# Local attention with a gated projection: softmax on halves of 64 query rows

## The chip, the cores and the metric

The kernel runs on one core of one Trainium2 chip. The metric is device time of one execution in microseconds (us). The engines are named as the profile names them: PE is the matrix engine (PEld its weight loads), DVE the vector engine, ACT the scalar engine, POOL the GpSimd engine, SP the queue that issues every DMA. PSUM is the memory that PE writes; it has eight banks of 512 fp32 columns, of which POOL can read none. SBUF is the other on-chip memory.

## What is computed

Attention for 4 batches, 8 heads, 768 positions, head size 64, in which a query sees the first 8 keys ("global") and the last 96 up to itself ("local"), with a bias by distance; then a causal convolution of five taps over positions makes a gate, and the gated projection is projected again.

```python
scores = scale * np.matmul(q, k.transpose(0, 1, 3, 2))
keep = is_global | is_local                       # key < 8, or 0 <= query - key < 96
scores = np.where(keep, scores + bias, -1000000000.0)
a = np.exp(scores - np.max(scores, axis=-1, keepdims=True))
a = a / (np.sum(a, axis=-1, keepdims=True) + 1e-09)
x = np.matmul(a, v)                               # heads side by side: 512 channels
gate = 1.0 / (1.0 + np.exp(-gate_pre))            # gate_pre: 5 causal taps over x
return (gate * (x @ w_val) @ w_out)
```

All inputs are fp32, the three weights are float64 in memory as the kernel gets them.

## The kernel before, in words

A **group** is one batch, one half of the sequence (`hf`, 384 positions) and one pair of heads; there are 32, in the order batch, half, pair. A group has three **steps** `k`, blocks of 128 queries; `s = 3 * g + k` numbers all 96. A step's window is 232 keys for all its 128 queries (96 before the block, 8 global, the block itself); the first step of a sequence needs only its own 128. So 80 steps are full and 16 are first steps.

A group passes through these operations, each a small function:

- `load`, `load_v0`, `load_v`: keys, queries and values by DMA, four buffers each. The window's values come as two tiles of 128 keys (`v`, 104 rows used of one).
- `scores` (S): for each step and head `j` one fp32 matmul, 64 rows of the array deep (head `j` lies on partitions 64 j to 64 j + 63), 128 queries wide, 232 keys long, into four PSUM banks `s`. A matmul has two records in the trace.
- `add_bias` (AM, DVE): scores plus bias to SBUF, with the row minimum. `expo` (EX, ACT): exp and row sum. `guard` (RG) and `recip` (RC): 1 / sum. `norm` (NM, POOL or DVE): the product.
- `transpose` (PT, PE): the probabilities `p` by matmul with the identity into one PSUM bank `pt`: for a full step two of 104 columns and two of 128. `evac_pt` (EV, ACT or DVE): to SBUF as `a`, 464 columns.
- `pv` (PV, PE): per head one matmul over 128 keys and one over 104 into the PSUM bank `x`; head `j` gets columns 64 j to 64 j + 63 of the array.
- `hist_in` (HI) puts the last four positions of the earlier half before `x`; `x_high` and `x_low` (XH, XL) split x into two reduced-precision parts `xh`, `xl`; `conv` (CV) runs five taps on x into `gate`; HO keeps the last four positions for the later half.

There is one bank `x`. For the first `EARLY` = 7 groups, `x_out` (XE) copies x to an SBUF tile `xs` at once, and the taps, XH and XL read that; POOL may then do some of them. From group 7 on they read the bank, which stays taken until they are done.

Four groups make a phase: `sigmoid`, `val` (projection, 48 matmuls of 384 columns), `gated` with `g_high` and `g_low`, `outp` (36 matmuls of 512 columns), `evac_o`, `store`. The eight weight slices are converted from float64 on the way, in about the first 25 steps: `f64_abs` (ACT), then `f64_op` 0 to 4 (operation 0, a clamp, on POOL or DVE; the rest on DVE), `w_high`, `w_rest`, `w_low`.

The order on every engine is fixed when the program is built. A planner (`Plan.order`) keeps for each operation an urgency (in units of steps; the constants `U_...`), the engines that may do it, each with a cost, and what it waits for, and hands out the operations one by one. `plan.ring` makes an operation wait until the n-th older user of a buffer has freed it. `PV` of a group and `S` of the group two later stand together on PE.

Of the kernel before, what the change touches and what calls it, by code (L numbers as in the profile page):

```python
# [8 lines left out]
F32 = mybir.dt.float32  # L9
# [5 lines left out]
ALU = mybir.AluOpType  # L15
AX = mybir.AxisListType
WARM = 8
S_B, PT_B, X_B = 4, 1, 1
# [8 lines left out]
EARLY, XS_B, U_XO, U_CVE = 7, 8, 0.21, 0.5  # L27
# [23 lines left out]
S_AT = {(k, j): (2 * j + k // 2, k % 2) for k in range(3) for j in range(2)}  # L51
# [79 lines left out]
def attention_moe(ctx, tc, qT, kT, kg, vw, v0, v, counts_in, wv, cw, wo, out):  # L131
# [39 lines left out]
    bias = one.tile([P, H, P + WIN], F32, name="bias")  # L171
# [8 lines left out]
    hist = one.tile([P, NP, HIST], F32, name="hist")  # L180

# [18 lines left out]
    def width(s):  # L200
        g, k = divmod(s, HB)
        return P if groups[g][1] == 0 and k == 0 else WIN
# [14 lines left out]
    def load_v(g):  # L217
        b, hf, p = groups[g]
        t = tile_of(("v", g), [P, HB, 2, 2, D], F32, "v", V_B)
        if hf == 0:  # L220
            nc.sync.dma_start(t[:, 1:], vw[b, p, :, : HB - 1])
        else:
            nc.sync.dma_start(t, vw[b, p, :, HB - 1 :])

    for g, (b, hf, p) in enumerate(groups):
# [5 lines left out]
        if hf == 0:  # L231
# [4 lines left out]
        plan.add(key, 3 * g + U_LV + 0.1, {SP: 0.5}, lambda e, g=g: load_v(g),  # L236
                 plan.ring("v", V_B, key, [("PV", g)]), P * (HB - 1 + hf) * 4 * D * 4)
# [11 lines left out]
    plan.add(("WARM",), -100, {PE: 0.43 * WARM}, lambda e: zeros(WARM))  # L249
    for g in range(FILL_TO):  # L250
# [4 lines left out]
    def iotas(e):  # L255
# [7 lines left out]
        nc.gpsimd.tensor_copy(rel[:, CA + NG :], rel0[:, OWN_A:])  # L263
        nc.gpsimd.iota(col, pattern=[[1, P]], base=0, channel_multiplier=0, allow_small_or_imprecise_dtypes=True)
# [35 lines left out]
    def biases(e, h, part):  # L300

        cols = slice(0, P) if part == 0 else slice(P, P + WIN)
        engine(e).tensor_scalar(  # L303
            out=bias[:, h, cols], in0=dist[:, cols], scalar1=-8.0 * 2.0 ** -(h + 1), scalar2=1.0,
# [13 lines left out]
    def f64_op(e, raw, n, nm, k):  # L318
# [4 lines left out]
        if k == 0:  # L323
            engine(e).tensor_scalar(out=y, in0=y, scalar1=F64_MIN, scalar2=1.0, op0=ALU.max, op1=ALU.mult)
# [14 lines left out]
    OPS64 = (0.45, 0.5, 0.7, 0.5, 0.65)  # L339
# [29 lines left out]
    for i in range(2 * NC):  # L369
# [6 lines left out]
        for k in range(5):  # L376
# [5 lines left out]
            plan.add(key, u + 0.1 * k, {DVE: OPS64[k]} if k else {DVE: OPS64[k], POOL: 0.95},  # L382
# [570 lines left out]
```

## Time and profile before

| | |
|---|---|
| runs, us | 320.62, 321.60, 321.67: median 321.6 |
| profiled execution: span, first to last instruction | 319.6 us; no other time is given of it |
| median less span | 2.0 us |
| busy share of the span | PE 90%, PEld 72%, DVE 73%, ACT 73%, POOL 54% |
| mean granted clock of PE | 0.960 |
| the chain that ended last, by engine | PE 59%, DVE 14%, POOL 13%, ACT 4%, no visible wait 4%, DMA 3% |
| DMA | 36.27 MB, 114 GB/s on average |

The busy shares are averages over stages with different limits; the slices of part 2 of the page tell the stages apart. A busy PE is not a PE at its peak: records of matmuls overlap. In the chain of waits a row tells when a piece began, how long it held the end up, and on which line. Groups of instructions are listed as line, engine, operation, output and inputs, shapes and count, then busy time and the mean of one, then the engine's idle time before them.

### The profile page before, as it was taken

Reading aid. Unit: us, or ns where it says so; the run is one execution under the profiler, and the core shown is the slowest. Engines: PE = TensorE matmul, PEld = TensorE weight load, DVE = VectorE, ACT = ScalarE, POOL = GpSimd, SP = SyncE. Lnnn points to the kernel's source line nnn. Section 1 sums busy time; section 2 is a strip of 40 time slices with the busy share of each in tenths; the row PEclk is TensorE's granted clock in tenths of the full one; section 3 lists DMA queues with packets and bytes.
Section 4 is the critical chain, followed back from the end, with each engine's and each line's share of the span. In section 5 each row is a group of like instructions: output and inputs, shape, how many; then the busy total and the mean of one; then the engine's idle time right before and its main releaser. Section 6 shows DMA issues by size and latency. Waiting matters only on the chain.

```text
span 319.6 us, 6850 instructions
## 1 busy us (share of the span) xinstructions
PE 286.8 (90%) x2140; PEld 230.8 (72%) x2140; DVE 232.5 (73%) x806; ACT 232.8 (73%) x650; POOL 173.4 (54%) x337
## 2 busy tenths in 40 slices
PE   6596886777689999999999999999999999999991
PEld 2363665665478987897789788987788778977980
DVE  4787678887758877698678876877697877995310
ACT  3596775877568977997789788967797779774220
POOL 5889999999982743454335434353435432641220
PEclk9697897899979999999999999999999999999998
DMA  6677536222314345522334344333443121001111
GB/s 188 245 243 269 152 123 171 67 85 83 91 67 132 110 115 155 163 84 83 123 126 150 114 144 142 118 83 93 138 159 105 54 82 70 0 3 61 40 47 63
DMA packets 21069, 36.27 MB, mean 114 GB/s; under 512 B 2592, under 2 KB 12832, under 8 KB 21024
## 3 DMA queue, kind: packets, MB, share of 16 engines
q1 hardware_dynamic: 21024, 35.75, 35.9%
q8 instruction: 19, 0.31, 0.4%
q14 instruction: 26, 0.21, 0.2%
HBM read 29.45 MB, written 6.29 MB: 112 GB/s over the span
## 4 chain that ended last, share of the span: by engine, by line
PE 59%; DVE 14%; POOL 13%; ACT 4%; issue 4%; DMA 3%; SPq 1%; POOLq 0%; ACTq 0%
PE o L682 16%; PE val L662 15%; PE s L433 7%; POOL p L466 7%; PE x L506 5%; DVE gate L603 5%; PE pt L479 4%; PE pt L482 4%; PE x L509 4%; DVE t L441 3%; PE pt L476 2%; DMA w<-in_wv 2%; ACT p L451 2%; PE x L502 1%; DVE xl L595 1%
## 5 line engine op out<-in xcount | busy, mean ns | idle before, releaser
L451 ACT ACTIVATE p<-t,mins 128x232 f32<-128x232 f32 (+1 forms) x192 | 90.4, 472 | 20.7 <-DVE mins L441 15.2
L466 POOL TENSOR_SCALAR p<-p,rs 128x232 f32<-128x232 f32 (+1 forms) x164 | 85.8, 534 | 32.4 <-DVE rs L461 17.0
L441 DVE CUSTOM_DVE_ANT_0 t<-s,bias 128x232 f32<-128x232 f32 (+1 forms) x192 | 69.6, 373 | 0.1
L603 DVE SCALAR_TENSOR_TENSOR gate<-x,cwt,gate 128x384 f32<-128x384 f32 x100 | 61.4, 614 | 5.6 <-ACT gate L605 5.3
L458 POOL TENSOR_SCALAR sm<-sm 128x2 f32<-128x2 f32 x88 | 19.3, 219 | 77.3 <-ACT p L451 72.3
L153 ACT COPY a<-pt 128x464 f32<-128x464 f32 (+1 forms) x90 | 46.2, 514 | 19.8 <-PE pt L482 16.8
L662 PE MATMUL val<-xh,wvh 128*128 128x384 f32 x128 | 46.9, 367 | 2.2 <-DVE g L669 2.2
L433 PE MATMUL s<-rk,rq 64*128 64x232 f32 (+1 forms) x384 | 44.8, 361 | 3.6 <-DVE bias L303 2.9
L662 PE MATMUL val<-xl,wvh 128*128 128x384 f32 x128 | 43.8, 342 | 2.9 <-POOL xl L595 2.9
L662 PE MATMUL val<-xh,wvl 128*128 128x384 f32 x128 | 43.8, 342 | 0.0
L682 PE MATMUL o<-woh,gh 128*128 128x512 f32 x96 | 41.8, 435 | 0.8 <-DVE g L669 0.7
L479 PE MATMUL pt<-ident,p 104*128 104x104 f32 x160 | 32.8, 277 | 9.3 <-POOL p L466 8.3
L675 POOL TENSOR_TENSOR gl<-g,gh 128x384 fp32r<-128x384 f32 x30 | 30.3, 1010 | 18.5 <-ACT gh L153 17.9
L479 PEld LDWEIGHTS pt<-ident,p 104*128 104x128 f32 x160 | 20.5, 145 | 27.4 <-POOL p L466 14.7
L682 PE MATMUL o<-wol,gh 128*128 128x512 f32 x96 | 38.3, 399 | 1.3 <-POOL wol L359 1.3
L433 PEld LDWEIGHTS s<-rk,rq 64*128 64x128 f32 x384 | 32.3, 186 | 9.5 <-DVE bias L303 3.4
L682 PE MATMUL o<-woh,gl 128*128 128x512 f32 x96 | 38.2, 398 | 0.0
L461 DVE RECIPROCAL rs<-sm 128x2 f32<-128x2 f32 x96 | 15.7, 164 | 29.6 <-POOL sm L458 28.4
L451 ACT ACTIVATION_READ_ACCUMULATOR p<-t,mins 128x1 f32 x192 | 36.4, 189 | 0.0
L506 PE MATMUL x<-a,v 128*64 128x128 f32 x320 | 33.0, 285 | 0.0
L482 PE MATMUL pt<-ident,p 128*128 128x128 f32 x160 | 32.2, 283 | 0.0
L509 PE MATMUL x<-a,v 104*64 104x104 f32 x320 | 28.8, 258 | 0.0
(176 smaller groups left out, 513.4 us busy)
## 6 DMA issues: line engine op xcount, KB each, us to landing
rq<-in_qT SPq DMA_DIRECT2D x32, 192.0 KB, 3.5
v<-in_vw SPq DMA_DIRECT2D x16, 384.0 KB, 3.2
out<-ob SPq DMA_DIRECT2D x24, 256.0 KB, 2.2
v<-in_vw SPq DMA_DIRECT2D x16, 256.0 KB, 2.7
rk<-in_kT SPq DMA_DIRECT2D x16, 252.0 KB, 3.6
rk<-in_kT SPq DMA_DIRECT2D x16, 200.0 KB, 3.4
w<-in_wv SPq DMA_DIRECT2D x4, 512.0 KB, 4.4
w<-in_wo SPq DMA_DIRECT2D x4, 512.0 KB, 3.7
```

Source lines behind the costliest of these rows:

```text
L153: nc.scalar.copy(dst, src)
L433: nc.tensor.matmul(T["s", g, k, j][:, :n], T["rq", g][r, k * P : (k + 1) * P], T["rk", g][r, c0 : c0 + n], start=True, stop=True)
L441: nc.vector.tensor_tensor_reduce(out=t[:, :n], in0=T["s", s // HB, s % HB, j][:, :n], in1=bias[:, h, :P] if n == P else bias[:, h, P:], op ...
L451: nc.scalar.activation(T["p", s][:, j, :n], T["t", s, j][:, :n], AF.Exp, bias=mins[:, s, j : j + 1], scale=-1.0, accum_out=T["sm", s][:, j ...
L466: engine(e).tensor_scalar(out=pr, in0=pr, scalar1=rs, scalar2=1.0, op0=ALU.mult, op1=ALU.mult)
L479: nc.tensor.transpose(pt[:, j * QA : (j + 1) * QA], pr[:QA, j, :P], ident[:QA, :QA])
L482: nc.tensor.transpose(pt[:, c : c + P], pr[:, j, CA:], ident)
L506: nc.tensor.matmul(head(j, P), T["v", g][:, k, j, 1], a[:, 2 * QA + j * P : 2 * QA + (j + 1) * P], start=True, stop=False)
L509: nc.tensor.matmul(head(j, QA), T["v", g][:CA, k, j, 0], a[:CA, j * QA : (j + 1) * QA], start=False, stop=True)
L603: nc.vector.scalar_tensor_tensor(out=gt, in0=src, scalar=w, in1=gt, op0=ALU.mult, op1=ALU.add)
L662: nc.tensor.matmul(T["val", ph, m], (wvh, wvh, wvl)[r][:, c, m * P : (m + 1) * P], (T["xh", g], T["xl", g], T["xh", g])[r], start=(c == 0 ...
L682: nc.tensor.matmul(T["o", ph, k], (T["gh", ph, c], T["gl", ph, c], T["gh", ph, c])[r][:, cols], (woh, woh, wol)[r][:, c], start=(c == 0 an ...
```

## The change

Each block of 128 queries is cut into two halves of 64. A half sees 168 keys: 104 that both halves see (32 before the block, the 8 global, the block's first 64) and 64 of its own ("far": the 64 before those for the first half, the block's last 64 for the second). All tiles of a step get 168 columns for 232.

- `scores`: per full step six matmuls for two. Each has 64 rows and 64 columns of the array, so a step uses four quarters: head by half. They go over 168, 104 and 64 keys. Two PSUM banks (one per head) for four.
- Head 0 keeps its shared keys first and head 1 its far keys first, so that in the row of 2 x 168 columns the far keys of both heads lie side by side. `transpose`: three of 128 columns for four (two for first steps, as before), into two banks in turn; `evac_pt` copies 384 columns for 464.
- `pv`: per head one matmul over the shared keys (128 columns of output) and two over the far keys (64 each). The shared values `vs` are padded with zero rows to 128. The far values `vo` lie in tiles in which the other head's rows are zero; those are cleared once at the start, on DVE (`VZ`). Three DMAs per group bring the values, for one.
- Two banks `x` for one; `EARLY`, `x_out` and the `xs` tiles go. HI, XH, XL and the taps read and write PSUM in all groups, so POOL does none of them.
- The clamp of the weights (`f64_op` 0) is on DVE alone. Some planner costs change; the urgencies stay.
- The layouts of v made before the launch follow; the window of distances gets two more pieces on POOL.

```diff
-S_B, PT_B, X_B = 4, 1, 1
+S_B, PT_B, X_B = 2, 2, 2
-EARLY, XS_B, U_XO, U_CVE = 7, 8, 0.21, 0.5
...
+QH = P // 2
+SH = WIN - 2 * QH
+SW = SH + QH
...
-        t = tile_of(("v", g), [P, HB, 2, 2, D], F32, "v", V_B)
+        t = tile_of(("vs", g), [P, HB, 2, D], F32, "vs", V_B)
+        nc.sync.dma_start(t[:, own], vs[b, p, :, blocks])
+        for j in range(2):
+            nc.sync.dma_start(vo_t[g % V_B][j * QH : (j + 1) * QH, j, own], vo[b, p, j, :, blocks])
...
+    def clear_v(e):
+        for t in vo_t:
+            for j in range(2):
+                nc.vector.memset(t[(1 - j) * QH : (2 - j) * QH, j], 0.0)
...
         if k == 0:
-            engine(e).tensor_scalar(out=y, in0=y, scalar1=F64_MIN, scalar2=1.0, op0=ALU.max, op1=ALU.mult)
+            ve.tensor_scalar(out=y, in0=y, scalar1=F64_MIN, scalar2=1.0, op0=ALU.max, op1=ALU.mult)
...
-        banks = [tile_of(("s", g, i), [P, 2, P * 2], F32, "s", S_B, psum) for i in range(4)]
+        banks = [tile_of(("s", g, j), [P, 4 * P], F32, "s", S_B, psum) for j in range(2)]
+            if n == P:
+                parts = [(0, 0, 0, c0, P), (1, 1, 0, c0, P), (0, 1, 0, c0, P), (1, 0, 0, c0, P)]
+            else:
+                c0 -= TAIL
+                parts = [(0, 1, 0, c0 + QH, SW), (1, 0, 0, c0, SW), (0, 0, 0, c0 + QH, SH), (1, 1, QH, c0 + QH, SH),
+                         (0, 0, SH, c0, QH), (1, 1, 0, c0 + SW, QH)]
+            for j, half, u, c, w in parts:
+                r = slice(j * D, (j + 1) * D)
+                s = T["s", g, k, j] = banks[j][:, k * SW : (k + 1) * SW]
+                rows = slice(half * QH, (half + 1) * QH)
+                nc.tensor.matmul(s[rows, u : u + w], T["rq", g][r, k * P + half * QH : k * P + (half + 1) * QH],
+                                 T["rk", g][r, c : c + w], start=True, stop=True)
...
-            for j in range(2):
-                nc.tensor.transpose(pt[:, j * QA : (j + 1) * QA], pr[:QA, j, :P], ident[:QA, :QA])
-            for j in range(2):
-                c = 2 * QA + j * P
-                nc.tensor.transpose(pt[:, c : c + P], pr[:, j, CA:], ident)
+        pr = T["p", s].rearrange("p two n -> p (two n)")
+        starts = (0, SW) if width(s) == P else (0, 2 * SW - P, SH)
+        for i, c in enumerate(starts):
+            nc.tensor.transpose(pt[:, i * P : (i + 1) * P], pr[:, c : c + P], ident)
...
+            for j in range(2):
+                nc.tensor.matmul(head(j, 0, P), T["vs", g][:, k, j], a[:, j * P : (j + 1) * P], start=True, stop=False)
+            for h in range(2):
+                for j in range(2):
+                    nc.tensor.matmul(head(j, h * QH, QH), far[:, j, k, h], a[:, 2 * P + h * QH : 2 * P + (h + 1) * QH],
+                                     start=False, stop=h == 1)
...
-    def x_out(e, g):
-        copy(e, T["xs", g][:, HIST:], T["x", g][:, HIST:])
...
-        x = tile_of(("xs", g), [P, HIST + HT], F32, "xs", XS_B) if g < EARLY else x_bank(g)
+        x = tile_of(("x", g), [P, HIST + HT], F32, "x", X_B, psum)
...
-        gt, src, w = T["gate", ph][:, p], x_of(g)[:, k : k + HT], cwt[:, p, k : k + 1]
+        gt, src, w = T["gate", ph][:, p], T["x", g][:, k : k + HT], cwt[:, p, k : k + 1]
...
-        xl = {DVE: 0.5}
-        plan.add(key, u + U_XH + 0.1, {POOL: 1.0, **xl} if early else xl, lambda e, g=g: x_low(e, g),
+        xl = {DVE: 0.48}
+        plan.add(key, u + U_XH + 0.1, xl, lambda e, g=g: x_low(e, g),
```

Two places show how this moves the instructions. The first is PE around the scores of group 15, in the middle of the run: the last step of PV, then S, then the first transposes. Before:

```order
L506 MATMUL x_2036<-a_1980,v_1553 64x128 x2
L509 MATMUL x_2036<-a_1980,v_1553 64x104 x2
L433 MATMUL s_0_2062<-rk_1569,rq_1578 128x232
L433 MATMUL s_2_2064<-rk_1569,rq_1578 128x232
L433 MATMUL s_0_2062<-rk_1569,rq_1578 128x232
L433 MATMUL s_2_2064<-rk_1569,rq_1578 128x232
L433 MATMUL s_1_2063<-rk_1569,rq_1578 128x232
L433 MATMUL s_3_2065<-rk_1569,rq_1578 128x232
L479 MATMUL pt_2080<-ident,p_1988 128x104 x2
L482 MATMUL pt_2080<-ident,p_1988 128x128 x2
```

Now, the last step of PV and the first of the three score steps:

```order
L516 MATMUL x_2053<-a_2162,vs_1693 64x128 x2
L519 MATMUL x_2053<-a_2162,vo_89 64x64 x4
L453 MATMUL s_0_2226<-rk_1716,rq_1727 64x168
L453 MATMUL s_1_2227<-rk_1716,rq_1727 64x168
L453 MATMUL s_0_2226<-rk_1716,rq_1727 64x104
L453 MATMUL s_1_2227<-rk_1716,rq_1727 64x104
L453 MATMUL s_0_2226<-rk_1716,rq_1727 64x64
L453 MATMUL s_1_2227<-rk_1716,rq_1727 64x64
```

The six score matmuls of a group become eighteen, alternating between the heads; a PV step goes from four matmuls to six. The second place is POOL in the first stage, about steps 6 to 9. Before (`p` is NM, `sm` the guard, `('w', 3)_y` the clamp of weight slice 3):

```order
L155 COPY xs_440<-hist 128x4
L466 TENSOR_SCALAR p_366<-p_366,rs_443 128x128 x2
L458 TENSOR_SCALAR sm_438<-sm_438 128x2
L466 TENSOR_SCALAR p_437<-p_437,rs_465 128x232 x2
L458 TENSOR_SCALAR sm_453<-sm_453 128x2
L324 TENSOR_SCALAR ('w', 3)_y<-('w', 3)_y 128x512
L466 TENSOR_SCALAR p_452<-p_452,rs_496 128x232 x2
L458 TENSOR_SCALAR sm_493<-sm_493 128x2
L466 TENSOR_SCALAR p_492<-p_492,rs_543 128x128 x2
L155 CAST xh_555<-xs_127 128x384
L458 TENSOR_SCALAR sm_531<-sm_531 128x2
L595 TENSOR_TENSOR xl_581<-xs_127,xh_555 128x384
```

Now, from the same step on:

```order
L486 TENSOR_SCALAR p_430<-p_430,rs_483 128x128 x2
L486 TENSOR_SCALAR p_468<-p_468,rs_498 128x168 x2
L478 TENSOR_SCALAR sm_525<-sm_525 128x2
L486 TENSOR_SCALAR p_524<-p_524,rs_563 128x168 x2
L478 TENSOR_SCALAR sm_557<-sm_557 128x2
L486 TENSOR_SCALAR p_556<-p_556,rs_593 128x128 x2
L478 TENSOR_SCALAR sm_597<-sm_597 128x2
L486 TENSOR_SCALAR p_596<-p_596,rs_635 128x168 x2
```

Between the normalisations stand no clamp, cast, copy or xl any more; only the guards are left.

More of the change, by code (lines that the diff above doesn't have):

```diff
@@ L170, in attention_moe @@
     d0, d1 = dist[:, :P], dist[:, P:]
-    bias = one.tile([P, H, P + WIN], F32, name="bias")
+    bias = one.tile([P, H, P + SW], F32, name="bias")
     wvh = const.tile([P, NC, DM], F32R, name="wvh")
@@ L180, in attention_moe @@
     hist = one.tile([P, NP, HIST], F32, name="hist")
+    vo_t = [one.tile([P, 2, HB, 2, D], F32, name=f"vo{i}") for i in range(V_B)]
     G = slice(CA, CA + NG)
@@ L201, in width @@
         g, k = divmod(s, HB)
-        return P if groups[g][1] == 0 and k == 0 else WIN
+        return P if groups[g][1] == 0 and k == 0 else SW
     def load(g, which):
@@ L300, in biases @@
     def biases(e, h, part):
-        cols = slice(0, P) if part == 0 else slice(P, P + WIN)
+        first = 0 if part == 0 else P + (QH if h % 2 == 0 else 0)
+        cols = slice(0, P) if part == 0 else slice(P, P + SW)
         engine(e).tensor_scalar(
-            out=bias[:, h, cols], in0=dist[:, cols], scalar1=-8.0 * 2.0 ** -(h + 1), scalar2=1.0,
+            out=bias[:, h, cols], in0=dist[:, first : first + (P if part == 0 else SW)], scalar1=-8.0 * 2.0 ** -(h + 1), scalar2=1.0,
             op0=ALU.mult, op1=ALU.mult,
@@ L381, in attention_moe @@
                 deps += plan.ring("wr", WT_B, key, [("WP", i)])
-            plan.add(key, u + 0.1 * k, {DVE: OPS64[k]} if k else {DVE: OPS64[k], POOL: 0.95},
+            plan.add(key, u + 0.1 * k, {DVE: OPS64[k]},
                      lambda e, i=i, k=k: f64_op(e, T["w", i], DM, ("w", i), k), deps)
@@ L556, in attention_moe @@
                     deps.append(("EX", s, 0))
-                plan.add(key, s + U_EX, {ACT: 0.48 if full else 0.39}, lambda e, s=s, j=j: expo(s, j), deps)
-            plan.add(("RG", s), s + U_RC - 0.1, {POOL: 0.16, DVE: 0.1}, lambda e, s=s: guard(e, s),
+                plan.add(key, s + U_EX, {ACT: 0.435 if full else 0.4}, lambda e, s=s, j=j: expo(s, j), deps)
+            plan.add(("RG", s), s + U_RC - 0.1, {POOL: 0.27, DVE: 0.2}, lambda e, s=s: guard(e, s),
                      [("EX", s, 0), ("EX", s, 1)])
@@ L647, in attention_moe @@
                 deps.append(("CV", g - 1, 0))
-            first = {DVE: 0.53, ACT: 0.5}
-            plan.add(key, u + (U_CVE if early else U_CV) + CV_STEP * k,
-                     {DVE: 0.58 if early else 0.53} if k else {POOL: 0.75, **first} if early else first,
+            plan.add(key, u + U_CV + CV_STEP * k, {DVE: 0.53} if k else {DVE: 0.53, ACT: 0.48},
                      lambda e, g=g, k=k: conv(e, g, k), deps)
@@ L898, in _window_rows @@
 def _window_rows():
-    rows = []
+    near, far = [], []
     for qb in range(1, NB):
         q0 = qb * P
-        first = list(range(q0 - TAIL, q0 + OWN_A))
-        rows.append([first + [q0] * (P - CA), list(range(NG)) + list(range(q0 + OWN_A, q0 + P))])
-    return rows
+        near.append([*range(q0 - TAIL + QH, q0 + OWN_A), *range(NG), *range(q0 + OWN_A, q0 + QH)])
+        far.append([[*range(q0 - TAIL, q0 - TAIL + QH)], [*range(q0 + QH, q0 + P)]])
+    return near, far
 def layouts(inputs):
```

128 lines of the change are left out of this document (49 added, 79 removed).

## The prediction

> **What bounds the kernel now.** I read the page's 40 slices first, then the chain of waits, then two stretches of busy time, then the groups by shape and tile.
>
> Page, part 2; one digit is the busy tenths of 8 us:
>
> ```profile
> PE   6596886777689999999999999999999999999991
> POOL 5889999999982743454335434353435432641220
> ```
>
> There are two stages. Until about 96 us (twelve digits) POOL is full and PE has holes; from 96 us PE is full and POOL half idle. The busy time of both stages (columns: stretch, length, then PE, PEld, DVE, ACT, POOL busy us with their instruction counts, clock, DMA) says the same:
>
> ```profile
> 8.00:96.00 88.00, 66.79 (x463) 49.49 (x465) 67.61 (x212) 62.67 (x180) 80.29 (x113) 0.86 0.45 145
> 96.00:300.00 204.00, 201.89 (x1599) 168.50 (x1596) 159.30 (x574) 164.19 (x459) 84.72 (x200) 1.00 0.34 104
> 48.00:56.00 8.00, 5.13 (x25) 4.45 (x22) 7.10 (x18) 4.39 (x12) 7.47 (x10) 0.73 0.59 170
> ```
>
> First stage: POOL 91%, DVE 77%, and PE at a granted clock of 0.86. Second: PE 99% at 1.00, nobody else over 81%. The chain of waits shows what that does to the pace of the score groups (start us, us, what):
>
> ```profile
> 9.79 1.95 POOL ('w', 0)_y L324
> 43.54 2.31 POOL ('w', 4)_y L324
> 59.00 1.38 PE s L433 x12
> 63.87 0.88 POOL gate L607
> 95.23 1.21 PE s L433 x12
> 102.56 1.21 PE s L433 x12
> 144.62 1.38 PE s L433 x12
> 267.93 1.38 PE s L433 x12
> 296.26 7.98 PE val L662 x45
> 304.25 8.40 PE o L682 x36
> ```
>
> The groups at 59.00 and 95.23 are numbers 6 and 9: 12.1 us a group. Those at 102.56 and 267.93 are 10 and 30: 8.27 us a group. So POOL sets the first pace and PE the second, and the end is a PE backlog: what the second stage saves on PE comes off the end in full, and what the first saves in time does too, as both stages keep the same matrix work.
>
> **The second stage, on PE.** The same chain gives the attention's PE prices, here around group 23 (columns as above):
>
> ```profile
> 209.09 0.18 PE pt L479 x2
> 209.27 0.22 PE pt L482 x2
> 210.01 0.37 PE x L506 x4
> 210.38 0.18 PE x L509 x4
> 210.56 0.22 PE x L506 x4
> 215.55 0.53 DVE gate L603
> 218.12 0.37 PE x L506 x4
> ```
>
> Scores. A group with three full steps takes 1.38 us, one whose first step is 128 wide takes 1.21. The 0.17 is 104 columns of one pair of heads, so a column of a pair costs 1.63 ns and a full step 232 x 1.63 = 0.38; 0.24 per group is fixed. The heads of a pair use different rows of the array. After, a step is six matmuls on four quarters of the array, and each quarter streams 168 columns in all. If all four run at once, a step is 168 x 1.63 = 0.27 (saves 0.11). If they start strictly in the order written, the first's two passes take 0.14, the next pair's second pass and the 64-column passes follow, 0.085 + 0.085 + 0.05: 0.36 (saves 0.02). If two quarters run at a time, 336 x 1.63 = 0.55 (costs 0.17). I take a saving of 0.08: the rows for x show two column halves side by side, those for s two row halves, but no row shows both, and passes of 64 columns leave little to hide a weight load behind.
>
> The Trainium skill has a rule for each side. Its page TensorEngine Tiling (Key Properties) lets different tiles load weights and multiply in parallel, four of them at 64 by 64; its page TensorE: Matmul & The Clock Gate (The mechanism) says that matmuls keep strict program order in start and end. By the first a step would be the 0.27 above, by the second the 0.36; no run here has a step of four quarters.
>
> Transposes. Two of 104 take 0.18 and two of 128 take 0.22, so 0.40 a step. Three of 128 are 3 x 0.11 = 0.33: saves 0.07, with no bound worth carrying, as the same instruction stands in the row.
>
> x. Two of 128 columns (four records) take 0.22, two of 104 take 0.18: 0.40 a step. After: two of 128 and four of 64. If 64 columns cost half of 128, 0.44 (costs 0.04). If a pair of 64 costs as much as the pair of 104, the nearest row, 0.22 + 2 x 0.18 = 0.58 (costs 0.18). I take 0.06, nearer to scaling, since 104 against 128 scales (0.18 to 0.22).
>
> Groups 10 to 31 hold 56 full steps and 10 first steps, which stay as they are. Sum: 56 x (-0.08 - 0.07 + 0.06) = **-5.0 us**.
>
> This needs the second x bank. One bank is held from the x matmuls at 210.01 to the last tap's end at 216.08, and the next group's start at 218.12: 8.1 of the 8.27 us pace. With one bank, less PE work would just have waited there. The others fit: ACT's 164 us in 204 are 6.7 of every 8.27, and DVE's 159 are 6.5, before they lose anything.
>
> **The first stage, on POOL and DVE.** POOL's and DVE's groups in 8 to 96 us (columns: line, engine, operation, tiles, shapes and count | busy us, mean ns | idle before):
>
> ```profile
> L466 POOL TENSOR_SCALAR p<-p,rs 128x232 f32<-128x232 f32 x41 | 29.9, 739 | 2.9 <-DVE rs L461 1.8 <-PE pt L476 0.7 <-PE pt L482 0.4
> L466 POOL TENSOR_SCALAR p<-p,rs 128x128 f32<-128x128 f32 x9 | 5.7, 644 | 0.8 <-PE pt L482 0.7
> L595 POOL TENSOR_TENSOR xl<-xs,xh 128x384 fp32r<-128x384 f32 x6 | 7.2, 1200 | 0.3
> L607 POOL TENSOR_SCALAR gate<-xs,cwt 128x384 f32<-128x384 f32 x3 | 2.6, 870 | 0.1
> L324 POOL TENSOR_SCALAR ('w', 4)_y<-('w', 4)_y 128x512 f32<-128x512 f32 x1 | 2.3, 2330 | 0.0
> L324 POOL TENSOR_SCALAR ('w', 1)_y<-('w', 1)_y 128x512 f32<-128x512 f32 x1 | 1.9, 1917 | 0.4 <-ACT ('w', 1)_y L316 0.4
> L355 POOL TENSOR_TENSOR ('w', 4)_h<-('w', 4)_h,woh 128x512 f32<-128x512 f32 x1 | 1.3, 1274 | 0.0
> L303 POOL TENSOR_SCALAR bias<-dist 128x232 f32<-128x232 f32 (+1 forms) x6 | 2.0, 357 | 0.2
> L603 DVE SCALAR_TENSOR_TENSOR gate<-xs,cwt,gate 128x384 f32<-128x384 f32 x28 | 20.9, 747 | 0.4 <-POOL gate L607 0.3
> L324 DVE TENSOR_SCALAR ('w', 2)_y<-('w', 2)_y 128x512 f32<-128x512 f32 x1 | 0.4, 424 | 0.0
> ```
>
> And over the whole run, by shape:
>
> ```profile
> L466 POOL TENSOR_SCALAR p<-p,rs 128x232 f32<-128x232 f32 x134 | 72.5, 552 | 23.0 <-DVE rs L461 14.0 <-DVE x L584 2.6 <-PE x L509 2.0
> L603 DVE SCALAR_TENSOR_TENSOR gate<-x,cwt,gate 128x384 f32<-128x384 f32 x100 | 61.4, 614 | 5.6 <-ACT gate L605 5.3
> L441 DVE CUSTOM_DVE_ANT_0 t<-s,bias 128x232 f32<-128x232 f32 x160 | 61.0, 392 | 0.1
> L441 DVE CUSTOM_DVE_ANT_0 t<-s,bias 128x128 f32<-128x128 f32 x32 | 8.7, 280 | 0.0
> L595 DVE TENSOR_TENSOR xl<-x,xh 128x384 fp32r<-128x384 f32 x25 | 13.9, 556 | 15.0 <-ACT gate L605 11.9 <-ACT hist L153 2.5 <-PE s L433 0.6
> ```
>
> POOL loses seven clamps of a weight (about 2.0 each, 14.2), six xl (7.2), three first taps (2.6) and some 2.5 of small copies and casts, since it cannot read the x that now stays in PSUM. It gains two more weight halves (1.3 each) and four biases (0.36 each): 4.0. The 41 full normalisations narrow by 64 columns at 0.9 ns ((739 - 644) / 104): 2.4. From 80.3 to about 55 of 88 us: no longer the bound.
>
> DVE gains seven clamps (0.42: 3.0) and six xl (0.56: 3.3). It loses 28 x (747 - 614) = 3.7 on taps that read PSUM, and 43 x 0.07 = 3.0 on the bias adds (392 to 280 over 104 columns is 1.08 ns, times 64), and about 2 of copies and weight halves that go elsewhere. 67.6 becomes about 65. So DVE is next. In its densest 8 us (48 to 56, above) it was 89% busy; at that share 65 us of work take 73, which would save 15. Groups 6 to 9 at the second stage's pace instead of 12.1 us would alone save 11.5. The other end is no gain, if dependencies keep DVE at 77%. On the chain seven POOL links vanish, from the clamp at 9.79 to the first tap at 63.87, 8.7 us in all; two clamps, three xl and two taps in their place (0.42, 0.56, 0.61) cost 3.7. I take **-9 us**, between the 5 that this leaves and the 15.
>
> Where the edits cost nothing: the eight clears of vo run on DVE while it waits for the counts, the two added iota pieces on POOL end before DVE asks for them (waits: who for whom, us in total, times, longest):
>
> ```profile
> DVE cf L275 <- DMA counts_i<-in_counts: 3.7, 1, 3.7
> POOL bias L303 <- DVE dist L288: 2.5, 1, 2.5
> SPq L221 <- PE x L509: 59.9, 11, 9.4
> ```
>
> Uncovered, each clear at most the 0.42 of a clamp, they would reach 0.4 past that wait. The two more DMA issues per group on SP queue ahead of the next key and query loads; those go out far ahead, and the v loads wait there for a free buffer anyway (the third row), so I price them at 0, at most 1 us at the start.
>
> **Sum.** 319.6 (span) - 5.0 - 9 = 305.6. The runs' median lies 2.0 over the span of the profiled execution: **307.5 us**.
>
> **The rivals.**
>
> 1. *DVE takes POOL's place at once* and the first stage keeps its length, but for 1 us. For it: 77% busy, with short instructions that wait for each other, may be all that it gives. Against it: 89% in one stretch. 319.6 - 5.0 - 1 + 2 = 315.5.
> 2. *Scores start in the order written* (the 0.36 above): 0.02 saved a step for 0.08, so 56 x 0.06 = 3.4 less is saved: 311.
> 3. *Everything opens*: the first stage saves the 15, and scores and x the full 0.11 and 0.04: -7.8. For it: POOL's p takes 739 ns in the first stage and 552 over the whole run, so (72.5 - 29.9) / 93 = 458 later, when the taps read x from PSUM; with xs gone it may be 458 from the start. 319.6 - 22.8 + 2 = 299. (The Trainium skill's page SBUF — State Buffer, section Who interferes with whom, has a rule by which a DVE instruction with two SBUF inputs and a reading GpSimd instruction exclude each other; the 747 against 614 and 739 against 458 agree.)
> 4. *Slower: the four quarters don't overlap.* Quarters that share a PSUM bank or a row half run one after the other, 0.17 dearer a step, and 0.21 in a first step (two pairs of 128 for one). From group 10 on, where PE has no idle time: 56 x (0.17 - 0.07 + 0.06) + 10 x 0.21 = +11; the first stage gives 4 at most as PE is slower there too. 319.6 + 7 + 2 = 328.5.
> 5. *Short x matmuls are bound by their weight loads* (0.18 for 0.06): 56 x 0.12 = 6.7 more: 314.
>
> **How the numbers follow.** Chances: forecast 0.40, rivals in order 0.14, 0.12, 0.14, 0.12, 0.08. All but the fourth are faster at their centre; the first and fifth each may lose the rest of their gain to costs priced at nothing, which I count as a third of their 0.22, split between no change and slower. With 0.3% (1 us) as what a measurement of this kernel tells from no change: faster 0.77, same 0.07, slower 0.16. The range 297.5 to 320 leaves out the fourth rival and the low half of the third.
>
> **What would show it.** Four overlapping quarters: the chain's rows of s (twelve records now, 36 then) become about 1.0 us a group (1.9 if they don't, 1.3 in order). Transposes: 0.33 a step; x: 0.44. POOL under 65% in the first stage and DVE over 85%; groups 6 to 9 at 10 us apart. Two banks: xh of one group while the next group's x matmuls run. I am wrong if score groups grow, if groups before the tenth stay 12 us apart, or if PE shows idle time after 96 us behind DVE or ACT.

## The result

The changed kernel takes 303.7 us (median of 4 runs, 301.99 to 303.91), the kernel before 321.1 (4 runs): a ratio of 0.945, 95% interval 0.942 to 0.948. The forecast was 307.5. The span of the profiled execution falls from 319.6 to 302.0 us.

Part 2 of the page of the changed kernel, a digit for 7.5 us:

```profile
PE   8688886989999999989998999999998999999991
POOL 4846569399334443345155432455145522550220
```

POOL has three slices of nine tenths instead of eight in a row, and PE's row is 9s with a few 8s from 68 us on (from 96 before). The busy time of two stretches, of the same form as in the prediction:

```profile
8.00:82.00 74.00, 62.95 (x733) 48.48 (x734) 65.71 (x236) 59.56 (x188) 50.49 (x101) 0.93 0.57 176
82.00:285.00 203.00, 196.92 (x2265) 166.74 (x2264) 142.55 (x553) 153.91 (x463) 81.37 (x206) 1.00 0.33 103
```

The first stage: POOL 68% (from 91), DVE 89% (from 77), and PE at a granted clock of 0.93 (from 0.86); whether the clock has a part in the gain wasn't tried. The second: PE 97%, 6.1 us without PE work where the kernel before had 2.1. Where the time came from is read from the starts of the score groups, here groups 9, 10 and 30 by the timeline of PE (start us, length):

```profile
78.36 1.02 PE L453 MATMUL s<-rk,rq 64*64 64x128 f32 x32
85.68 1.02 PE L453 MATMUL s<-rk,rq 64*64 64x128 f32 x32
250.62 1.11 PE L453 MATMUL s<-rk,rq 64*64 64x168 f32 x36
```

Group 10 starts at 85.7 instead of 102.5, groups 10 to 30 take 164.9 us instead of 165.4, and from group 30 to the end it is 51.4 instead of 51.7. So 16.8 of the 17.6 us come from the first stage (9 were forecast) and 0.8 from the second (5.0 were forecast). Of the 16.8 some is work put off: before group 10 PE has done 51 matmuls of `val` where the kernel before had done 57, and 6 x 0.17 = 1.0 us of PE work comes later. Yet PE's prices fell as forecast, or better. The chain of waits has the score groups, and the timeline of PE the x steps:

```profile
191.78 1.04 PE s L453 x24
198.83 0.95 PE s L453 x27
```

```profile
149.16 0.39 PE L516 MATMUL x<-a,vs 128*64 128x128 f32 x4
149.38 0.40 PE L519 MATMUL x<-a,vo 128*64 128x64 f32 x8
149.61 0.39 PE L516 MATMUL x<-a,vs 128*64 128x128 f32 x4
```

A group of three full steps takes 1.04 us for its scores (1.38 before), one with a first step 0.95 (1.21). An x step starts 0.45 us after the one ahead of it (0.40 before), and transposes keep their 0.11 each, three instead of four. In groups 10 to 29 (ten of three full steps, ten of two) that is 10 x 0.34 + 10 x 0.26 of scores and 50 x 0.07 of transposes, less 50 x 0.05 of x: 7.0 us of PE work less. (`val` and `outp` hardly change it: 237 and 177 matmuls there for 234 and 180.) It shortened this stretch by 0.5 us. The same stretch of both kernels, first of before, then of the changed kernel:

```profile
102.50:267.90 165.40, 163.54 (x1314) 135.86 (x1312) 128.85 (x479) 137.22 (x397) 73.62 (x175) 1.00 0.39 116
```

```profile
85.70:250.60 164.90, 158.89 (x1901) 133.73 (x1899) 119.14 (x471) 130.48 (x400) 68.01 (x174) 1.00 0.38 118
```

PE's idle time grew from 1.9 to 6.0 us: 4.1 of the 7.0. Another 2.4 went into time that still counts as busy. Nobody else is near full: ACT 79%, DVE 72%.

### The profile page after: what moved, and what is told of

It reads as the page before. It is cut to its first block, busy times and chain, and to the rows that moved or that the text cites. A ratio compares the mean times of both kernels' runs of the same rounds, so it can differ in the third digit from the quotient of the medians.

```text
span 302.0 us, 8865 instructions
## 1 busy us (share of the span) xinstructions
PE 276.7 (92%) x3084; PEld 226.5 (75%) x3084; DVE 214.9 (71%) x811; ACT 218.5 (72%) x658; POOL 138.5 (46%) x327
## 4 chain that ended last, share of the span: by engine, by line
PE 61%; DVE 16%; POOL 10%; ACT 5%; issue 3%; DMA 2%; SPq 1%; POOLq 0%; ACTq 0%
PE o L670 19%; PE val L650 15%; PE pt L494 7%; PE s L453 7%; PE x L516 5%; DVE gate L604 5%; POOL p L486 5%; PE x L519 5%; DVE t L461 3%; DVE xl L596 2%; DMA w<-in_wv 2%; DVE g L657 2%; DVE p L486 1%; ACT p L471 1%; PE x L513 1%
## 5 line engine op out<-in xcount | busy, mean ns | idle before, releaser
L471 ACT ACTIVATE p<-t,mins 128x168 f32<-128x168 f32 (+1 forms) x192 | 81.9, 429 | 20.9 <-DVE mins L461 19.6
L486 POOL TENSOR_SCALAR p<-p,rs 128x168 f32<-128x168 f32 (+1 forms) x170 | 73.9, 447 | 31.2 <-DVE rs L481 25.7
L494 PE MATMUL pt<-ident,p 128*128 128x128 f32 x272 | 54.3, 290 | 7.5 <-POOL p L486 5.6
L461 DVE CUSTOM_DVE_ANT_0 t<-s,bias 128x168 f32<-128x168 f32 (+1 forms) x192 | 59.2, 316 | 1.1 <-PE s L453 1.0
L494 PEld LDWEIGHTS pt<-ident,p 128*128 128x128 f32 x272 | 32.8, 141 | 24.7 <-POOL p L486 15.9
L154 ACT COPY a<-pt 128x384 f32<-128x384 f32 (+1 forms) x88 | 39.9, 455 | 7.1 <-PE pt L494 7.0
L453 PE MATMUL s<-rk,rq 64*64 64x104 f32 (+3 forms) x1088 | 37.7, 280 | 1.7 <-DVE mins L461 0.9
L481 DVE RECIPROCAL rs<-sm 128x2 f32<-128x2 f32 x96 | 15.6, 163 | 31.2 <-POOL sm L478 30.1
L453 PEld LDWEIGHTS s<-rk,rq 64*64 64x64 f32 x1088 | 32.9, 143 | 6.3 <-DMA rk<-in_kT 1.5
L519 PE MATMUL x<-a,vo 128*64 128x64 f32 x640 | 32.8, 225 | 0.0
L516 PE MATMUL x<-a,vs 128*64 128x128 f32 x320 | 32.8, 284 | 0.0
```

The lines of the kernel that those rows point to most:

```text
L154: nc.scalar.copy(dst, src)
L453: nc.tensor.matmul(s[rows, u : u + w], T["rq", g][r, k * P + half * QH : k * P + (half + 1) * QH], T["rk", g][r, c : c + w], start=True, s ...
L461: nc.vector.tensor_tensor_reduce(out=t[:, :n], in0=T["s", s // HB, s % HB, j][:, :n], in1=bias[:, h, :P] if n == P else bias[:, h, P:], op ...
L471: nc.scalar.activation(T["p", s][:, j, :n], T["t", s, j][:, :n], AF.Exp, bias=mins[:, s, j : j + 1], scale=-1.0, accum_out=T["sm", s][:, j ...
L486: engine(e).tensor_scalar(out=pr, in0=pr, scalar1=rs, scalar2=1.0, op0=ALU.mult, op1=ALU.mult)
L494: nc.tensor.transpose(pt[:, i * P : (i + 1) * P], pr[:, c : c + P], ident)
```

## The experiments

Three questions: what PE work of the second stage is worth at the end; what holds that stage if not PE; and which part of the change made the first stage. The table has all runs; the starts of groups are those of each profiled execution. The kernels ran on several chips, on which the median of the kernel before was 321.0 to 322.2 us; the ratios compare on the same chip, so differences of medians between two rows can be off by about 1 us.

| kernel | median, us | ratio to before (95%) | group 10 starts | groups 10 to 30 |
|---|---|---|---|---|
| before | 321.1 | | 102.5 | 165.4 |
| changed | 303.7 | 0.945 (0.942 to 0.948) | 85.7 | 164.9 |
| before, more transposes | 324.0 | 1.007 (1.004 to 1.009) | 102.8 | 167.2 |
| changed, more transposes | 305.4 | 0.948 (0.943 to 0.952) | 86.1 | 166.5 |
| before, fewer x matmuls | 318.8 | 0.989 (0.986 to 0.992) | 103.7 | 162.7 |
| before, tanh | 320.8 | 0.997 (0.995 to 0.999) | 102.8 | 164.5 |
| changed, tanh | 299.2 | 0.931 (0.926 to 0.935) | 84.3 | 161.9 |
| changed, exponentials ahead | 301.6 | 0.936 (0.933 to 0.938) | 85.4 | 163.4 |
| both of these | 300.8 | 0.934 (0.930 to 0.937) | 85.7 | 162.2 |
| changed, clamps on POOL | 316.3 | 0.984 (0.980 to 0.987) | 98.7 | 164.9 |
| before, clamps on DVE | 312.3 | 0.972 (0.970 to 0.974) | 93.9 | 165.5 |
| changed, one bank for x | 308.7 | 0.957 (0.953 to 0.962) | 94.9 | 160.9 |
| changed, one bank from group 8 | 302.5 | 0.942 (0.940 to 0.945) | 84.8 | 164.6 |
| the same with tanh | 300.9 | 0.938 (0.935 to 0.940) | 85.8 | 161.1 |

### PE work added and taken away

One transpose more in each full step from group 10 on, in both kernels (here the changed one):

```diff
-        for i, c in enumerate(starts):
+        again = [(2, SH)] if width(s) == SW and s >= 30 else []
+        for i, c in [*enumerate(starts), *again]:
```

For the kernel before:

> The same 56 extra transposes on the kernel before, 6.2 us of PE work. Both theories take PE as the bound of its second stage: it grows by 5 to 6.5 us. Less than 4 would say that the premise of the prediction, that PE work of the second stage goes to the end in full, was wrong already for the kernel before.

For the changed kernel:

> The changed kernel with one transpose more (0.11 us on PE) in each of the 56 full steps from group 10 on, into the same columns of the same bank: 6.2 us of PE work added, nothing else. Theory A: PE has holes (6.1 us without work between 82 and 285 us, and about 3 more hidden in the records of val), which take a good part: the run grows by 1 to 4 us. Theory B (PE is the bound): it grows by 5.5 to 6.5 us.

The kernel before grew by 2.1 us (1.4 to 2.8 by the interval), the changed one by 1.0 (ratios) or 1.8 (medians), at the low end of theory A. The premise fell for the kernel before already: 50 transposes in groups 10 to 29 are 5.5 us, and the stretch grew by 1.8 (changed kernel: by 1.6). The busy time says where the rest is, in the run of before with more transposes:

```profile
102.80:270.00 167.20, 166.29 (x1362) 141.49 (x1360) 128.85 (x479) 137.84 (x397) 74.04 (x175) 1.00 0.38 115
```

PE's busy time grew by 2.75 us (163.54 to 166.29) for 5.5 us of work, and its idle time fell by 0.95. So 2.75 us of the added work went into time that had counted as busy. How that can be is seen where val waits (timeline of PE, the changed kernel):

```profile
152.91 0.34 PE L650 MATMUL val<-xh,wvl 128*128 128x384 f32 x1
153.08 0.34 PE L650 MATMUL val<-xh,wvh 128*128 128x384 f32 x1
...
153.43 0.34 PE L650 MATMUL val<-xh,wvl 128*128 128x384 f32 x1
154.30 0.44 PE L650 MATMUL val<-xh,wvh 128*128 128x384 f32 x1 [0.53 <-ACT ob L154]
```

A val record is 0.34 us long, but the next one starts 0.17 after it when nothing holds it up. The last one here starts 0.87 later: 0.70 lost, of which 0.53 count as idle, and a hole below 0.17 would not count at all. The Trainium skill (Perfetto Trace Analysis, section Identifying the Most-Contended Engine) calls the busy share of matmuls no good measure of how close the engine is to its limit, because they are pipelined. This trace agrees that it is none, by the 2.75 us; the prediction had not drawn on it.

The other direction, in the kernel before:

```diff
-            for c, j in ((1, 0), (1, 1), (0, 1), (0, 0)):
+            less = s >= 30 and s % 2 == 1
+            for c, j in ((1, 0), (1, 1)) if less else ((1, 0), (1, 1), (0, 1), (0, 0)):
...
-                                     start=True, stop=False)
+                                     start=True, stop=less)
```

> The kernel before without the x matmuls of the 104 window keys in every second step from group 10 on (their part of x is left out): 28 pairs of 0.18 us, 5.0 us of PE work less, and nothing else. The premise of the prediction, that PE work of the second stage comes off the end in full, gives -5 us (groups 10 to 30 in 161 us for 165.4). The theory that the run with added transposes suggests, that PE's 99% hide waits of an in-order PE and only about 0.4 of a change of PE work reaches the end, gives -1 to -2 us.

Of the 28 pairs 22 lie in the stretch: 4.0 us of work. It fell by 2.7, the run by 3.3 (medians), between the two expectations. In sum, of a change of PE work in the second stage a third (added) to two thirds (removed) reaches the end. By these two runs the 7.0 us less of the changed kernel should have brought 2.3 to 4.7, not 0.5.

### The gate's activation

`sigmoid` needs another function table than the exponentials. With tanh it needs none (the copy of the output tile, not shown, multiplies by 0.5):

```diff
-        nc.scalar.activation(T["gate", ph], T["gate", ph], AF.Sigmoid)
+        nc.scalar.activation(T["gate", ph], T["gate", ph], AF.Tanh, scale=0.5)
...
-        nc.vector.tensor_mul(t, T["val", ph, m], T["gate", ph][:, m])
+        nc.vector.scalar_tensor_tensor(out=t, in0=T["gate", ph][:, m], scalar=1.0, in1=T["val", ph, m],
+                                       op0=ALU.add, op1=ALU.mult)
```

> The changed kernel with the gate's sigmoid written as (1 + tanh(x/2))/2, the half going into the copy of the output tile; the planner's costs and so the order of all else are as before. Tanh and the exponentials share one function table, so the two table loads of 1.28 us around each of the eight sigmoids vanish. Theory A (after 82 us the end is set by the stretch of 2.8 to 5 us in which ScalarE does a sigmoid with its two table loads and no exponential: POOL, DVE and then PE run dry behind it): the second stage gets back most of the 5 us that were forecast and did not come, score groups 10 to 30 take 160 us or less in place of 164.9, and the whole run is 295 to 299 us. Theory B (PE is still the bound of the second stage, its records merely have dearer gaps): groups 10 to 30 stay at 164 to 165 and the run takes 300 to 303 us.

> The same edit on the kernel before. Theory A: PE is 99% busy there from 96 us on and its backlog covers each sigmoid, so groups 10 to 30 stay within 0.7 us of 165.4 and the run keeps 317 to 321 us (only the sigmoid at 58 us lies in the first stage, worth at most its 2.6 us). A third theory C (ScalarE's total work sets both kernels): the run before falls by as much as the one after, 5 us or more.

The changed kernel gains 4.4 us by the medians, 3.0 of them in groups 10 to 30; the kernel before gains 1.0 (0.2 to 1.7), 0.9 of them there. So ScalarE's table loads cost the changed kernel's second stage three times what they cost before. That is 3.0 of the 4.9 us that theory A asked for (161.9 us, not 160, and PE is still without work for 3.6 us); theories B and C are out. In the kernel before the run stays in theory A's 317 to 321, but 0.9 is over its 0.7. What differs is in the stretches from one table load to the next. First the kernel before, then the changed one (windows, columns as above):

```profile
165.80:168.60 2.80, 2.80 (x32) 2.25 (x32) 2.02 (x11) 2.77 (x3) 0.72 (x2) 1.00 0.16 60
233.00:235.80 2.80, 2.80 (x37) 2.31 (x37) 2.57 (x7) 2.77 (x3) 0.92 (x3) 1.00 0.28 95
```

```profile
145.20:148.90 3.70, 3.68 (x18) 2.39 (x16) 0.65 (x3) 3.35 (x3) 0.58 (x2) 1.00 0.19 71
211.00:214.70 3.70, 3.68 (x16) 2.38 (x14) 0.67 (x4) 3.36 (x3) 0.59 (x2) 1.00 0.19 71
```

Before, DVE (third) works through the sigmoid; now it stands still, with 0.65 us of work in 3.7. Its queue goes on with a reciprocal (`rs`) that needs the sums of exponentials not yet made, and the taps stand behind it (timeline of DVE, changed kernel):

```profile
151.11 0.17 DVE L481 RECIPROCAL rs<-sm 128x2 f32<-128x2 f32 x1 [4.49 <-POOL sm L478]
```

The waits of the changed kernel between 82 and 285 us, and of before between 96 and 302, have the same row (who for whom, us in total, times, longest):

```profile
DVE rs L481 <- POOL sm L478: 25.8, 25, 4.5
```

```profile
DVE rs L461 <- POOL sm L458: 13.2, 18, 1.6
```

### The exponentials ahead of the output copy

The two rows of 3.7 us show one more thing. The timeline of ACT there, changed kernel:

```profile
211.01 1.28 ACT L643 ACT_TABLE_LOAD   x1
212.30 1.49 ACT L643 ACTIVATE gate<-gate 128x1536 f32<-128x1536 f32 x1
214.11 0.59 ACT L154 COPY ob<-o 128x512 f32<-128x512 f32 x1 [0.32 <-PE o L670]
214.71 1.28 ACT L471 ACT_TABLE_LOAD   x1
216.01 0.44 ACT L471 ACTIVATE p<-t,mins 128x168 f32<-128x168 f32 x1
```

The planner, with the new costs, set the copy of an output tile between the sigmoid and the next exponential; the copy waits for PE, and the table load stands behind it. It did so after the sigmoids at 116, 145 and 211 us (4.5, 3.7 and 3.7 us from load to load; 2.8 after all others and in the kernel before). So the rows of ACT were moved, after planning, and nothing else:

```diff
+        act = [m for m in range(n + 1, len(rows)) if rows[m][3] == "scalar"][:6]
+        oe = [m for m in act if key[rows[m][2]][0] == "OE"]
+        ex = [m for m in act if key[rows[m][2]][0] == "EX"][:2]
+        if oe and ex and oe[0] < ex[0]:
+            for m in ex:
+                rows.insert(oe[0], rows.pop(m))
+                oe[0] += 1
```

(`rows` is the finished order, `n` the place of a sigmoid in it.)

> The changed kernel with two exponentials moved ahead of the copy of an output tile on ScalarE in the three places (after the sigmoids at 116, 145 and 211 us) where the plan set that copy between a sigmoid and the next exponential; the table load for the exponentials then follows the sigmoid at once. No other instruction moves. If these three late returns (3.7 to 4.5 us between the two table loads instead of 2.8) make the hollows on PE that follow them, 0.9 to 1.7 us each come back: -1.5 to -3.5 us on the run, and PE idle time in the second stage falls by as much. If the hollows come from the sigmoids as such, or from the pace of a whole group's chain, the run gains less than 1 us.

The run gains 2.1 us by the medians (2.9 by the ratios), 1.5 in groups 10 to 30. So the three places are worth about that much. PE's idle time in groups 10 to 30 falls by 1.2 us (6.0 to 4.8), somewhat less than the run. With both edits, tanh and this one:

> The tanh gate and the exponentials ahead of the output copy together, in the order of the changed kernel. If the moved exponentials gained because a table load stood behind the copy, nothing is left to gain without table loads: within 1 us of the tanh kernel's 299.2 (ratio 0.931). If they gained because the chain of a group's softmax waited for PE's output tile through that copy, another 0.5 to 1.5 us comes off: 297.5 to 298.7 us.

300.8 against 299.2 for tanh alone, 1.6 us above it by the medians and 1.0 by the ratios, with intervals that overlap, and groups 10 to 30 within 0.3 us: without table loads the move gains nothing that these runs can tell. In the tanh kernel the copy still stands before the next exponential, and waits longer for PE than before:

```profile
210.58 0.60 ACT L679 ACTIVATE ob<-o 128x512 f32<-128x512 f32 x1 [1.76 <-PE o L671]
```

So it isn't the copy's wait for PE alone that cost, but the table load on top of it. Read the other way, tanh takes 0.8 us off the kernel with the exponentials ahead (1.2 in groups 10 to 30; the intervals overlap), about what it took off the kernel before (1.0 and 0.9). The three times dearer table loads of the changed kernel are, within what these runs tell, the three late returns.

### The clamps

`f64_op` 0 of all eight weights on POOL again, at the same place of the same order:

```diff
-            ve.tensor_scalar(out=y, in0=y, scalar1=F64_MIN, scalar2=1.0, op0=ALU.max, op1=ALU.mult)
+            nc.gpsimd.tensor_scalar(out=y, in0=y, scalar1=F64_MIN, scalar2=1.0, op0=ALU.max, op1=ALU.mult)
```

> The changed kernel with the eight clamps of the weights on POOL again, each at the same place of the same order (0.34 us on DVE becomes 1.2 to 2.3 us on POOL). Theory F1 (the clamps were a main part of what the first stage gained): group 10 starts 4 us or more later than 85.7 and the run grows by as much. Theory F2 (the copies of x, the first taps and xl that left POOL, and the second bank, carried it): group 10 starts less than 1.5 us later.

Theory F1: group 10 starts 13.0 us later, and the run is 12.7 us longer. (The clamps measure 0.40 to 0.56 us on DVE in the changed kernel and 1.91 to 1.92 on POOL here, not the 0.34 and 1.2 to 2.3 expected.) One of POOL's clamps between 8 and 96 us, the busy time and the waits of that stretch, in this run:

```profile
L337 POOL TENSOR_SCALAR ('w', 0)_y<-('w', 0)_y 128x512 f32<-128x512 f32 x1 | 1.9, 1918 | 0.9 <-ACT ('w', 0)_y L329 0.9
```

```profile
8.00:96.00 88.00, 67.36 (x738) 51.30 (x739) 65.09 (x230) 60.53 (x192) 65.75 (x110) 0.84 0.50 150
```

```profile
PEld pt L494 <- POOL p L486: 17.6, 20, 2.8
PE pt L494 <- POOL p L486: 12.3, 12, 2.7
DVE ('w', 1)_y L339 <- POOL ('w', 1)_y L337: 3.1, 1, 3.1
DVE ('w', 5)_y L339 <- POOL ('w', 5)_y L337: 3.0, 1, 3.0
DVE ('w', 0)_y L339 <- POOL ('w', 0)_y L337: 2.8, 1, 2.8
```

POOL is only 75% busy in this stretch, and DVE has fallen to 74%: neither is full, and it still is 13 us slower. Two waits grew. A clamp of 1.92 us stands in POOL's queue ahead of the normalisations, and PE's transposes wait for those: 12.3 us in 12 waits, where the changed kernel up to 82 us has 5.6 in 9:

```profile
PE pt L494 <- POOL p L486: 5.6, 9, 1.6
```

And DVE, the busiest engine of the changed kernel's first stage, has the next operation of the same weight at its old place in its queue and now stands still until POOL's clamp is done: 15.4 us in seven such waits, of which three are shown; with the clamp on DVE there are none. Its work is the same (65.1 us, 65.7 before the edit), and its time without work in the first stage rises by 14.6 us (22.9 of 88 for 8.3 of 74), about the loss. Which of the two waits made more of it no run separates. The order was planned for clamps on DVE, so the 13 us are the price of a clamp on POOL in that order, and not in one planned for it.

Then the same line alone in the kernel before, the other way round:

```diff
-            engine(e).tensor_scalar(out=y, in0=y, scalar1=F64_MIN, scalar2=1.0, op0=ALU.max, op1=ALU.mult)
+            ve.tensor_scalar(out=y, in0=y, scalar1=F64_MIN, scalar2=1.0, op0=ALU.max, op1=ALU.mult)
```

> The kernel before with one line of the change alone: the eight weight clamps on DVE, each at its place in the same order (seven of them leave POOL, where they take 1.9 to 2.3 us, for 0.42 us on DVE). Theory G1 (the clamps alone held the first stage, as the changed kernel with them on POOL again suggests: group 10 there starts 13.0 us later): group 10 starts 10 us or more earlier than 102.5, the run is 306 to 312 us. Theory G2 (in the kernel before, POOL stays full with the other work that the change takes from it: xl, first taps, wider normalisations): group 10 starts 2 to 6 us earlier, the run is 315 to 320 us.

Between the two: group 10 starts 8.6 us earlier, the run is 8.7 us shorter by the medians. The busy time of the first stage, in this run:

```profile
8.00:96.00 88.00, 74.54 (x532) 55.70 (x531) 77.10 (x249) 70.00 (x194) 68.65 (x110) 0.92 0.49 159
```

POOL, which was the full engine of the kernel before (91%), is at 78%, and DVE at 88%. DVE's waits for a clamp were short in the kernel before (3.3 us in three), which suggests that here it is mainly POOL's time that the line sets free. So one line of the change, added alone, makes half of its gain. The rest of the first stage's 16.8 us, 8.2, needs the rest of the change, whose parts but for the second bank weren't tried one by one.

### The second bank

One bank in the changed kernel; the planner makes a new order.

```diff
-S_B, PT_B, X_B = 2, 2, 2
+S_B, PT_B, X_B = 2, 2, 1
```

> The changed kernel with one PSUM bank for x in place of two and nothing in place of the other; the planner orders the work anew with that. Theory F2 (x without copies in SBUF needs the second bank): the x of a group waits until the taps of the group before are done, group 10 starts 4 us or more later and groups 10 to 30 take 167 us or more, the run is 310 us or more. Theory F1: the bank is worth under 3 us in all, 303 to 306 us.

Group 10 starts 9.2 us later, so without the copies the first stage needs the second bank (F2, and 308.7 us lies between the two expectations). The second stage takes 4.0 us less, against F2. 1.5 us of that is work of `val` already done, 9 matmuls of 0.17 us more than in the changed kernel before group 10. To see whether the rest is the bank or the order:

```diff
-                 plan.ring("x", X_B, key, last) + ([("HO", g - NP)] if hf else []))
+                 plan.ring("x", X_B, key, last) + ([("HO", g - NP)] if hf else []) + (taken if g >= 8 else []))
```

(`taken` is the `last` of the group before.)

> The changed kernel with both banks for x up to group 7, and from group 8 on with the rule of one bank (x of a group waits for the last tap of the group before), under which the planner made an order whose groups 10 to 30 took 160.9 us in place of 164.9. Theory H1 (the order that the planner makes with the second bank is what cost the second stage its gain): group 10 starts at 85 to 87 us, groups 10 to 30 take 160 to 162.5 us, the run is 298 to 301.5 us. Theory H2 (that gain came from the later first stage, which had done 9 matmuls of val more, 1.4 us of PE work, and from chance in the order): groups 10 to 30 take 163.5 us or more and the run 302 us or more.

Theory H2. Its second stage takes 164.6 us: the rule of one bank isn't what helped. Together with tanh, as above, and the planner told of the shorter hold:

```diff
-        plan.add(("SG", ph), u + U_SG, {ACT: 4.0}, lambda e, ph=ph: sigmoid(ph),
+        plan.add(("SG", ph), u + U_SG, {ACT: 1.5}, lambda e, ph=ph: sigmoid(ph),
```

> after_mix with the tanh gate as well, and with the planner told that the gate's activation holds ScalarE for 1.5 us instead of 4.0. If both gains are of different places (the order of the groups, ScalarE's table loads): 294 to 297 us, groups 10 to 30 in 158 to 160 us. If both only fill the same waits of PE: 297 to 300 us.

300.9, the same as tanh and exponentials together, and slower than tanh alone by 1.7 us; just outside the second expectation. The rule of one bank had brought the second stage next to nothing by itself (164.6 for 164.9), so there was little to add, and the planner made another order with the new cost: the run doesn't tell whether two gains fill the same waits. The order that one bank gave is better by some 2.5 us in the second stage, and why stays open.

In the second stage the second bank is hardly used. The timeline of the changed kernel, around an end of the taps and the next group's x:

```profile
196.11 0.62 DVE L604 SCALAR_TENSOR_TENSOR gate<-x,cwt,gate 128x384 f32<-128x384 f32 x1
197.25 0.44 PE L516 MATMUL x<-a,vs 128*64 128x128 f32 x4
```

The last tap has been over for 0.5 us when the next x starts. In groups 10 to 30 only three of 21 start their x while the last tap of the group before still runs or waits, and by then that group's `xh` is long done: the prediction's sign of two banks, `xh` beside the next group's x matmuls, isn't seen there.

## Why the prediction was right or wrong

**Right: the direction, and PE's prices.** Four quarters of the array at once is what the rows show: 1.04 us a group, where 1.3 would have been the order as written (rival 2) and 1.9 no overlap (rival 4). The step was taken at -0.08 and measured -0.11, the bound; first steps, priced as unchanged, fell by (0.26 - 0.23) = 0.03. By the Trainium skill's page TensorEngine Tiling (Array Packing), section Key Properties, different tiles can load weights and multiply in parallel, and the step of 0.38 - 0.11 = 0.27 agrees. (The 0.36 of rival 2 counts 0.14 for two passes of 168 columns, which are 0.27 at the prediction's own price; dearer, that rival would be further off.) Transposes -0.07 as forecast; x +0.05 for 0.06, so rival 5 (0.18) is out.

**Right by chance: the total.** The two terms erred in opposite directions. 16.8 for 9 and 0.8 for 5.0 give 17.6 for 14.0. (Two sums of the prediction are slightly off: 305.6 + 2.0 is 307.6, and a third of 0.22 split between no change and slower makes the chances 0.81 faster, 0.04 same and 0.16 slower, not 0.77, 0.07 and 0.16.)

**First stage: the term of -9 was mis-sized.** The working had the right end. DVE did take POOL's place, at 89% (65.7 us in 74), and "65 us of work take 73" came out near that. Rival 1 (DVE holds the old length) is out. What failed is the choice between the bounds, drawn down by the chain, on which only two clamps stand (8.7 - 3.7 = 5 for all its links). The 16.8 lies even over the upper bound of 15; 1.0 of it is the work of `val` put off. The clamp runs show what the chain left out: seven clamps (14.2 us of POOL's work) taken off POOL in the kernel before gave 8.7, where the chain has two, 4.3 us. What an operation on the full engine costs was not to be read from the links of it that stand on the chain.

Groups 6 to 9 are 10.3 us apart, as foreseen (12.1 before). POOL was foreseen under 65% and is at 68.

**Second stage: the step that failed is "PE bound, so what it saves on PE comes off the end in full".** It rested on PE's 99% busy at full clock. The runs with more and with less PE work show that in the kernel before a third to two thirds of a change reaches the end: 2.3 to 4.7 of the 7.0 us. The late exponentials in the order that the planner made with the new costs took 1.5 of that back in this stretch, by the run that moves them. With the 0.5 that came, 0.3 to 2.7 us are left without a cause that a run shows; the order alone was worth 2.5 in the run with one bank. What else holds the second stage wasn't found as one engine: taking 15.6 us of ACT's work away (tanh, in the changed kernel) gave 3.0, taking 4.0 of PE's (in the kernel before) gave 2.7. The prediction named the sign of it (idle time of PE after 96 us behind DVE or ACT), but gave it no price: ACT at 6.7 and DVE at 6.5 of every 8.27 us were taken for room. These means hid that ACT makes no exponential for 4.1 us or, at the three late returns, for 5.0 to 5.8 from the first table load of a sigmoid on (211.01 to 216.01 in the rows above).

**The second bank: "With one bank, less PE work would just have waited there" was a misreading.** The 8.1 of 8.27 us ran from x to the next x. By the rows quoted there the bank was free from 216.08 to 218.12, 2 us before the next group took it. It was not what the second stage waited for, and with one bank that stage ran no slower.

**Costs priced at nothing** were small, but not nothing at the start. The eight clears take 3.85 us, 0.48 each for "at most the 0.42", and the first use of the counts stands behind them in DVE's queue: it comes at 4.67, where the kernel before, waiting for the DMA, has it at 3.70. That is 1.0 past that wait for the 0.4 foreseen (DVE's timeline: the changed kernel, then before):

```profile
0.89 3.85 DVE L256 MEMSET vo<- 64x384 f32 x8 [0.89 <-PEq L935]
4.67 0.10 DVE L287 CAST cf<-counts_i 128x4 f32<-128x4 int32 x1
```

```profile
3.70 0.17 DVE L275 CAST cf<-counts_i 128x4 f32<-128x4 int32 x1 [3.70 <-DMA counts_i<-in_counts]
```

Group 1 starts 4 us later than before (14.0 for 9.8), but group 4 is ahead again; the cause of that late start, and what the 1.0 us is worth at the end, weren't tried.

Rival 3 (everything opens, 299) had the prices and the first stage right, and missed where the second stage's 7 us stay.

## What to carry to other kernels

Before pricing a saving on an engine that is "99% busy", add a known piece of work to it and see how much reaches the end: in the kernel before it was a third to two thirds. After a change of costs, read the new order around the rare long instructions (a sigmoid with its two table loads, a clamp of 1.9 us) and ask which in-order queue stands behind each. A consumer of the long instruction on another engine waits as well: DVE stood still 15.4 us for clamps moved to POOL. And run each line of a change alone: the one about the clamp made half of the gain.

The fastest kernel here is the changed one with the tanh gate: 299.2 us, 0.931 (0.926 to 0.935) of before, and 4.4 us below the changed kernel by the medians.

## What the runs showed of the hardware

Four 64 by 64 quarters of the array run at once in fp32: a step of six short matmuls takes 0.11 us less than two long ones on two row halves, although it has three times as many weight loads (1.04 us for a group's scores, 1.38 before; 168 columns at the 1.63 ns of the old rows are the 0.27 of a step).

A table load takes 1.28 us and, in the rows above, the next activation starts 0.01 to 0.02 us after it: 1.28 a switch. The Trainium skill (ScalarE: Activation LUTs, section What ACT_TABLE_LOAD costs) adds a drain of about 1.38; no run here shows one. Tanh shares the exponentials' table, as that page's section on table sets says: one table load is left in the run with it, and its activation takes 1.49 us, as the sigmoid's. ACT's groups there:

```profile
L643 ACT ACTIVATE gate<-gate 128x1536 f32<-128x1536 f32 x8 | 11.9, 1488 | 1.2 <-DVE gate L604 1.2
L281 ACT ACT_TABLE_LOAD x1 | 1.3, 1283 | 0.7 <-PEq L940 0.7
```

POOL's normalisation, narrowed from 232 to 168 columns, takes 549 ns in the first stage, where the wider took 739, and 461 over the whole run:

```profile
L486 POOL TENSOR_SCALAR p<-p,rs 128x168 f32<-128x168 f32 x42 | 22.6, 549 | 7.3 <-DVE rs L481 5.9 <-PE s L453 0.7 <-PE pt L494 0.4
```

Narrowing alone would give 739 - 64 x 0.9 = 681 by the prediction's price of a column; what made the rest wasn't tried.
